# Fused attention and two feed-forward layers: transposes behind later weight loads, another order of seven products, a shorter alternation at the end

## The chip, the cores and the metric

The kernel runs on one core of one Trainium2 chip. The metric is device time in microseconds of one launch; three runs before gave 1210.41, 1207.80 and 1208.92, median 1208.92.

## The reference

What is computed, cut to its core (scale factors of the inputs left out):

```python
# q, k, v: (8, 8, 576, 64); chunks of 64 rows attend to themselves alone
scores = (1/8) * q_c @ k_c.T
attn = exp(scores - max) / (sum + 1e-9)
x = heads_side_by_side(attn @ v_c)              # (4608, 512)
h = x @ w_in                                    # (512, 2048)
x = (h / (1 + exp(-h))) @ w_out                 # (2048, 512)
h = x @ w_in2                                   # (512, 1024)
e = exp(h - max(h)); solu = h * e / (sum(e) + 1e-9)
ln = (solu - mean) / sqrt(var + 1e-6) * g_ln
out = ln @ w_out2                               # (1024, 512)
```

## The kernel before

The 4608 rows are worked in nine blocks of 512. Every factor of a large product is kept as two float16 parts, high and low, and a product is three matmuls: high x high, high x low, low x high. Blocks 0 and 1 run while the weights are still being decoded and split; from block 2 on the large products use a scheme in which four quarter products become seven products of sums (Strassen's), so each layer runs seven products j = 0 to 6 on operands that VectorE, ScalarE and GpSimd prepare, and puts the results together in `combine` (L485). There `a`, `c[0]` and `p` are PSUM banks, named pa, pb and pc in the profile. Product 0 goes into pa and is copied out by ScalarE (L494); product 1 is added on top in pa and copied (L501); product 3 goes into pb and is copied (L498); product 4 goes into pc and is added by VectorE; product 2 goes on top of pa, 6 on top of pb, 5 on top of pa. The order of the seven is a tuple: `HSEQ = (0, 3, 1, 4, 2, 6, 5)` or `XSEQ = (0, 4, 1, 3, 2, 6, 5)`.

A block b from 3 on has these stages on TensorE:

- First half: the first layer for one half of the hidden columns (`h_fast` twice, alternately), 14 products of 12 matmuls (lines L479 to L481), operands x and xb. Each product takes one tile of the weight ring.
- The second layer of the block before for its second pair of row tiles, `m_fast(b - 1, 1)` (L666), alternating with the output product of the first two row tiles, `m_out` (lines L790, L791 and L798).
- Second half: `h_fast` twice again, then `m_out` of the third row tile, and, from here on called the x phase, the seven products of the first layer's second matrix (`x_fast`, lines L580 to L582) with the attention of the next block between them (s_ps, x_ps) and `m_out` of the fourth row tile after the first product.
- Beside the last product of the x phase, piece by piece: `m_fast(b, 0)`, the second layer for the block's own first pair (lines L696 to L698). Its operands are xs[0] = x2q of quarter (0, c), xs[4] and xs[5] = x2q of quarter (1, c), and xs[1], xs[2], xs[3], xs[6] = the sums x2s that VectorE and ScalarE make of both (`x_fast`, L610 to L613, split at L108 and L113).

`m_fast` ends in `m_norm` (L728), the softmax and layer norm of a pair of row tiles: exp (L752), its product (L754), squares (L760), a power on GpSimd (L767), scaling (L770), the two parts of u (L771 on ScalarE, L772 on VectorE), and then four DMA transposes uT<-u (L776) on the sync queue, two for each row tile. `m_out` reads uT.

The weight ring (`Ring`, L438) holds eight tiles of 256 KB. After each product `load` issues the load of the tile that goes into the slot just freed (L449). The loads, the transposes and all other DMAs named here are issued by SyncE, in the order in which they stand in its program; one that waits holds those behind it. A block takes 56 ring tiles: 28 of the first matrix (w1s) and 28 of the second (w2s). The order of instructions on each engine is found by a scheduler from the order in the code, dependences and priorities.

At the end, after the last block, `m_fast(8, 1)` alternates with the rest of the third output tile and the whole fourth one of block 7; then the four output tiles of block 8 follow.

Of the kernel before, what the change touches and what calls it, by code (L numbers as in the profile page):

```python
# [16 lines left out]
P = 128  # L17
# [29 lines left out]
def fused(ctx: ExitStack, tc: tile.TileContext, qkv, w1, w2, w3, w4, g_ln, out):  # L47
    nc = tc.nc
    V, A, G, T = nc.vector, nc.scalar, nc.gpsimd, nc.tensor
# [13 lines left out]
    MO = (0, 1, 2, 3)  # L63
# [3 lines left out]
    EXB = [6, 7, 10, 13, 14]  # L67
    PHA = [4, 5, 6, 7, 8, 10, 11, 15, 32, 33, 34, 35]
    QF = 14

    const = ctx.enter_context(tc.tile_pool(name="const", bufs=1))
    one = ctx.enter_context(tc.tile_pool(name="one", bufs=1))
# [340 lines left out]
    UL = V  # L413
# [13 lines left out]
    def w2_sums(c, q):  # L427
        ys = [one.tile([P, 2, 4, P], F32, tag=f"q{10 + i}", name="y") for i in range(2)]

        def staging():  # L430
# [4 lines left out]
        sums((w2t[c, q], w2t[c, 2 + q], w2t[2 + c, q], w2t[2 + c, 2 + q]),  # L435
             lambda j: dst[j], [ys[i // 2][:, i % 2] for i in range(4)], staging)

    class Ring:  # L438


# [4 lines left out]
        def load(self):  # L445
            while self.n < min(self.used + self.depth, self.count):
                shape, src = self.src(self.n)
                t = one.tile(shape, F16, tag=f"{self.tag}_{self.n % self.depth}", name="ring")
                nc.sync.dma_start(out=t, in_=src)  # L449
                self.tiles.append(t)  # L450
                self.n += 1

        def take(self):
            self.used += 1
# [10 lines left out]
    HSEQ = (0, 3, 1, 4, 2, 6, 5)  # L465
# [18 lines left out]
    def combine(h, shape, seq, product, done, add, c21_first=False):  # L484

        a, c = bank(shape, "pa"), {}  # L490
        for j in seq:
            if j == 0:
                product(j, a, True)
                A.activation(h[0], a, AF.Copy)  # L494
            elif j == 3:
                c[0] = bank(shape, "pb")
                product(j, c[0], True)
                A.activation(h[3], c[0], AF.Copy)  # L498
            elif j == 1:
                product(j, a, False)  # L500
                A.activation(h[1], a, AF.Copy)  # L501
            elif j == 4:
                p = bank(shape, "pc")
                product(j, p, True)
                add(0, h[0], p)
                done(0, 0, h[0])
            elif j == 2:
                product(j, a, False)
                add(3, h[3], a)
                done(1, 1, h[3])  # L510
            elif j == 6:
                product(j, c[0], False)
                add(1, h[1], c[0])
                if c21_first:
                    done(1, 0, h[1])
            else:
                product(j, a, False)
                done(0, 1, a)
                if not c21_first:
                    done(1, 0, h[1])  # L520
            yield

    def run(*parts):

        parts = list(parts)
        while parts:
            for g in list(parts):
                if next(g, parts) is parts:
                    parts.remove(g)
# [147 lines left out]
    def m_fast(b, c, alt=False):  # L677

        e, tags = [], []
        for i in range(2):  # L680
            if b < NB - 1:
                tags.append(e_tag(ns[0]))
                ns[0] += 1
            else:
                tags.append(f"q{4 + 2 * c + i}")
            e.append(one.tile([P, F2], F32, tag=tags[i], name="e"))
        z = xq.pop((b, 2, c))
        x0, x1 = xq.pop((b, 0, c)), xq.pop((b, 1, c))
        a, d = slice(0, P), slice(P, HB)
        xs = ([x0[:, i, :, a] for i in range(2)], [y[:, 1] for y in z], [y[:, 0] for y in z], [y[:, 2] for y in z],  # L690
              [x1[:, i, :, a] for i in range(2)], [x1[:, i, :, d] for i in range(2)], [y[:, 3] for y in z])

        def product(j, ps, start):
            (h, l), w = xs[j], w3s[j]
            for k in range(2):
                T.matmul(ps, h[:, k], w[:, 0, k], start=start and k == 0, stop=False, skip_group_check=True)  # L696
                T.matmul(ps, h[:, k], w[:, 1, k], start=False, stop=False, skip_group_check=True)
                T.matmul(ps, l[:, k], w[:, 0, k], start=False, stop=k == 1, skip_group_check=True)  # L698


        y = [e[i // 2][:, i % 2 * 512:i % 2 * 512 + 512] for i in range(4)]


        part = sml.tile([P, 2], F32, tag="mp", name="mp")
        m = sml.tile([P, 2], F32, tag="mm_", name="mm_")

        def add(n, out, p, own=True):
            i = n // 2
            first = n in (0, 3)
            V.tensor_tensor_reduce(  # L710
                out=out, in0=p, in1=out if own else zero.to_broadcast([P, 512]), scale=1.0,
                scalar=LEAST if first else part[:, i:i + 1], op0=ALU.add, op1=ALU.max,
                accum_out=(part if first else m)[:, i:i + 1])

        def done(r, k, x):
            if (r, k) == (0, 1):
                add(2, y[2], x, own=False)

        yield from combine(y, [P, 512], HSEQ, product, done, add)
        u_tags, uT_tags = ["m1", "w3_10"], [tags[0] if c else "m2", tags[1]]  # L720
        if alt:
            u_tags, uT_tags = ["q0", "q2"], ["q1", "q3"]
        elif not more_(b):
            uT_tags = ["q10", "q11"]
        m_norm(b, [2 * c, 2 * c + 1], [[(e[i], slice(0, F2))] for i in range(2)], m, e, u_tags, uT_tags,
               G if alt else UL)

    def m_norm(b, ts, parts, m, es, u_tags, uT_tags, eng_l=V):  # L728

        n, np = len(ts), len(parts[0])  # L730
        us_ = [one.tile([P, 2, F2], F16, tag=x, name="u") for x in u_tags]
        small = lambda tag: sml.tile([P, n], F32, tag=f"{tag}{n}", name=tag)
        inv = 1.0 / (S_X2 * S_W)

        def joined(tag, one_part):

            r = sml.tile([P, n * np], F32, tag=f"{tag}{n}", name=tag)
            for i in range(n):
                for k, (y, c) in enumerate(parts[i]):
                    one_part(i, y, c, r[:, i * np + k:i * np + k + 1])  # L740
            if np == 1:
                return r
            z = sml.tile([P, n], F32, tag=f"{tag}j", name=tag)
            V.tensor_reduce(out=z, in_=r, axis=AX.X, op=ALU.add)
            return z

        nm = small("nm")
        for i in range(n):
            V.tensor_scalar(out=nm[:, i:i + 1], in0=m[:, i:i + 1], scalar1=-inv, scalar2=None, op0=ALU.mult)
        ex = [u.rearrange("p h f -> p (h f)").bitcast(F32) for u in us_]  # L750
        s = joined("s", lambda i, y, c, r: exps.append(
            A.activation(ex[i][:, c], y, AF.Exp, scale=inv, bias=nm[:, i:i + 1], accum_out=r).ins))  # L752

        us = joined("us", lambda i, y, c, r: V.scalar_tensor_tensor(  # L754
            out=es[i][:, c], in0=y, scalar=1.0, in1=ex[i][:, c], op0=ALU.mult, op1=ALU.mult, accum_out=r))
        nmu = small("nmu")
        V.tensor_scalar(out=nmu, in0=us, scalar1=-1.0 / F2, scalar2=None, op0=ALU.mult)
        dv = small("dv")
        for i in range(n):
            A.activation(ex[i], es[i], AF.Square, bias=nmu[:, i:i + 1], accum_out=dv[:, i:i + 1])  # L760


        V.tensor_scalar(out=s, in0=s, scalar1=1e-9, scalar2=1.0 / inv, op0=ALU.add, op1=ALU.mult)
        c = small("c")
        V.scalar_tensor_tensor(out=c, in0=s, scalar=1e-6 / S_LN ** 2, in1=s, op0=ALU.mult, op1=ALU.mult)
        V.scalar_tensor_tensor(out=c, in0=dv, scalar=1.0 / F2 / S_LN ** 2, in1=c, op0=ALU.mult, op1=ALU.add)  # L766
        G.tensor_tensor(out=c, in0=c, in1=mhalf.to_broadcast([P, n]) if n > 1 else mhalf, op=ALU.pow)  # L767
        for i in range(n):
            e, u = es[i], us_[i]
            V.tensor_scalar(out=e, in0=e, scalar1=nmu[:, i:i + 1], scalar2=c[:, i:i + 1], op0=ALU.add, op1=ALU.mult)  # L770
            A.activation(u[:, 0, :], e, AF.Copy)  # L771
            eng_l.tensor_tensor(out=u[:, 1, :], in0=e, in1=u[:, 0, :], op=ALU.subtract)  # L772
            uT = one.tile([P, 2, K2, P], F16, tag=uT_tags[i], name="uT")
            ut[b, ts[i]] = uT[:, 0], uT[:, 1]
            for h in range(2):
                nc.sync.dma_start_transpose(out=uT[:, h], in_=u[:, h])  # L776

    def in_turn(*parts):
        for g in parts:
            yield from g  # L780
# [207 lines left out]

    b = NB - 1
    run(begun)  # L990
    run(m_fast(b, 1), in_turn(m_out(b - 1, MO[2], high=False), m_out(b - 1, MO[3])))
    for t in MO:
        run(m_out(b, t))

# [46 lines left out]
```

## Time and profile before

| | |
|---|---|
| median of the timed runs | 1208.92 us (1207.80 to 1210.41) |
| the profiled execution | 1211.81 us |
| its span, first to last instruction | 1210.0 us |
| TensorE busy | 1137.6 us (94%) |
| VectorE busy | 906.0 us (75%) |
| ScalarE busy | 805.5 us (67%) |
| mean granted TensorE clock | 0.978 of full speed |

The times in the views count from the start of the span. "Idle before" an instruction is the time its engine stood still, with what released it. PE is TensorE, DVE VectorE, ACT ScalarE, POOL GpSimd, SP SyncE; a q behind the name is the engine's queue.

### The profile page before, as it was taken

Reading aid. Unit: us, or ns where it says so; the run is one execution under the profiler, and the core shown is the slowest. Engines: PE = TensorE matmul, PEld = TensorE weight load, DVE = VectorE, ACT = ScalarE, POOL = GpSimd, SP = SyncE. Lnnn points to the kernel's source line nnn. Section 1 sums busy time; section 2 is a strip of 40 time slices with the busy share of each in tenths; the row PEclk is TensorE's granted clock in tenths of the full one; section 3 lists DMA queues with packets and bytes.
Section 4 is the critical chain, followed back from the end, with each engine's and each line's share of the span. In section 5 each row is a group of like instructions: output and inputs, shape, how many; then the busy total and the mean of one; then the engine's idle time right before and its main releaser. Section 6 shows DMA issues by size and latency. Waiting matters only on the chain. (4 is left out here: it accounts for less than half of the span.)

```text
span 1210.0 us, 23575 instructions
## 1 busy us (share of the span) xinstructions
PE 1137.6 (94%) x9036; PEld 770.7 (64%) x9036; DVE 906.0 (75%) x1638; ACT 805.5 (67%) x1475; POOL 251.8 (21%) x241
## 2 busy tenths in 40 slices
PE   4997889988999989999999999999999999999998
PEld 4444434444557766787678766867677767777853
DVE  5888986568587788788878887778688867886343
ACT  7777767766577668746875687558755875587243
POOL 3356423224201430032003200311021102100001
PEclk7898979999999999999999999999999999999999
DMA  8778643444446655676567666666666667564704
GB/s 290 247 228 247 202 144 104 128 152 131 128 110 199 180 170 157 183 207 186 158 183 207 187 157 183 194 184 163 168 200 199 166 150 216 176 157 138 205 15 113
DMA packets 205169, 209.18 MB, mean 173 GB/s; under 512 B 120192, under 2 KB 130432, under 8 KB 205056
## 3 DMA queue, kind: packets, MB, share of 16 engines
q1 hardware_dynamic: 205056, 207.68, 59.0%
q8 instruction: 70, 1.15, 0.4%
q14 instruction: 43, 0.35, 0.1%
HBM read 156.24 MB, written 24.12 MB: 149 GB/s over the span
## 5 line engine op out<-in xcount | busy, mean ns | idle before, releaser
L113 DVE SCALAR_TENSOR_TENSOR q<-hc,q 128x512 f16<-128x512 f32 x196 | 137.9, 719 | 12.5 <-ACT q L108 10.3
L108 ACT ACTIVATE q<-hc 128x512 f16<-128x512 f32 x196 | 120.2, 626 | 38.0 <-DVE hc L561 12.1
L112 POOL TENSOR_TENSOR qbl<-qk,qbh 64x512 f16<-64x512 f32 x58 | 79.7, 1374 | 283.0 <-ACT qbh L108 237.0
L580 PE MATMUL pa<-q,ring 128*128 128x256 f16 x448 | 122.7, 274 | 0.0
L581 PE MATMUL pa<-q,ring 128*128 128x256 f16 x448 | 122.7, 274 | 0.0
L582 PE MATMUL pa<-q,ring 128*128 128x256 f16 x448 | 122.7, 274 | 0.0
L790 PE MATMUL o_ps<-w4h,uT 128*128 128x512 f16 x288 | 109.2, 379 | 1.7 <-DMA uT<-u 1.7
L791 PE MATMUL o_ps<-w4l,uT 128*128 128x512 f16 x288 | 109.2, 379 | 0.0
L767 POOL TENSOR_TENSOR c<-c,mhalf 128x2 f32<-128x2 f32 (+1 forms) x22 | 14.1, 642 | 396.9 <-DVE c L766 396.9
L479 PEld LDWEIGHTS <-ring 128*128 128x128 f16 x784 | 77.0, 98 | 20.3 <-DMA ring<-w1s 9.7
L480 PEld LDWEIGHTS <-ring 128*128 128x128 f16 x784 | 77.0, 98 | 15.0 <-issue 4.5
L581 PEld LDWEIGHTS <-ring 128*128 128x128 f16 x784 | 76.9, 98 | 11.5 <-issue 0.3
L580 PEld LDWEIGHTS <-ring 128*128 128x128 f16 x784 | 76.9, 98 | 11.3
L481 PEld LDWEIGHTS <-ring 128*128 128x128 f16 x784 | 77.0, 98 | 9.1
L582 PEld LDWEIGHTS <-ring 128*128 128x128 f16 x784 | 76.9, 98 | 9.2
L798 PE MATMUL o_ps<-w4h,uT 128*128 128x512 f16 x288 | 70.3, 379 | 0.0
L479 PE MATMUL pa<-xb,ring 128*128 128x256 f16 x224 | 61.1, 273 | 8.9 <-DMA ring<-w1s 7.6
L479 PE MATMUL pa<-x,ring 128*128 128x256 f16 x224 | 61.3, 274 | 2.1 <-ACT hc L494 2.1
L481 PE MATMUL pa<-x,ring 128*128 128x256 f16 x224 | 61.5, 274 | 0.0
L480 PE MATMUL pa<-x,ring 128*128 128x256 f16 x224 | 61.3, 274 | 0.0
L479 PE MATMUL pb<-x,ring 128*128 128x256 f16 x224 | 61.1, 273 | 0.2 <-DMA ring<-w1s 0.2
L580 PE MATMUL pb<-q,ring 128*128 128x256 f16 x224 | 61.1, 273 | 0.0
(264 smaller groups left out, 3484.5 us busy)
## 6 DMA issues: line engine op xcount, KB each, us to landing
ring<-w1s SPq DMA_DIRECT2D x196, 256.0 KB, 3.3
ring<-w2s SPq DMA_DIRECT2D x196, 256.0 KB, 3.8
wst<-w SPq DMA_DIRECT2D x48, 512.0 KB, 4.9
qk<-qkv SPq DMA_DIRECT2D x29, 512.0 KB, 3.8
vs<-qkv SPq DMA_DIRECT2D x36, 256.0 KB, 3.1
out<-o SPq DMA_DIRECT2D x36, 256.0 KB, 2.1
w1s<-ws SPq DMA_DIRECT2D x32, 128.0 KB, 1.8
w2s<-ws SPq DMA_DIRECT2D x16, 256.0 KB, 2.0
```

What stands on the lines that cost most here:

```text
L108: A.activation(dst_h, src, AF.Copy, scale=scale)
L112: return G.tensor_tensor(out=dst_l, in0=src, in1=dst_h, op=ALU.subtract).ins
L113: return V.scalar_tensor_tensor(out=dst_l, in0=src, scalar=scale, in1=dst_h, op0=ALU.mult, op1=ALU.subtract).ins
L479: T.matmul(ps[:, c], wh, x[:, 0, k], start=first, stop=False, skip_group_check=True)
L480: T.matmul(ps[:, c], wh, x[:, 1, k], start=False, stop=False, skip_group_check=True)
L481: T.matmul(ps[:, c], wl, x[:, 0, k], start=False, stop=k == 1, skip_group_check=True)
L580: T.matmul(ps[:, c], wh, g[:, 0], start=first, stop=False, skip_group_check=True)
L581: T.matmul(ps[:, c], wh, g[:, 1], start=False, stop=False, skip_group_check=True)
L582: T.matmul(ps[:, c], wl, g[:, 0], start=False, stop=q == 1 and f == 3, skip_group_check=True)
L790: T.matmul(ps, uh[:, k], w4h[:, k, :], start=k == 0, stop=False)
L791: T.matmul(ps, uh[:, k], w4l[:, k, :], start=False, stop=False)
L798: T.matmul(ps, ul[:, k], w4h[:, k, :], start=False, stop=k == K2 - 1)
```

## The change

Three edits. First, for the second pair of a block (not of the last one) `m_norm` no longer issues the transposes where it stands; it puts them on a list `late`, and the ring issues the first tile's two right behind the load with which its count has grown by seven, and the second tile's two behind the load after that. Second, `m_fast` runs its seven products in the order XSEQ where it had HSEQ. Third, at the end `m_fast(8, 1)` alternates with the rest of the third output tile alone, and the fourth one comes behind it.

```diff
+    DEFER = 7
...
+    late = []
...
-                nc.sync.dma_start(out=t, in_=src)
+                i = nc.sync.dma_start(out=t, in_=src).ins
                 self.tiles.append(t)
                 self.n += 1
+                if late and late[0][0] <= self.n:
+                    with tc.issue_after(i):
+                        late.pop(0)[1]()
...
-        yield from combine(y, [P, 512], HSEQ, product, done, add)
+        yield from combine(y, [P, 512], XSEQ, product, done, add)
...
         m_norm(b, [2 * c, 2 * c + 1], [[(e[i], slice(0, F2))] for i in range(2)], m, e, u_tags, uT_tags,
-               G if alt else UL)
+               G if alt else UL, DEFER if c and more_(b) else 0)
...
-            for h in range(2):
-                nc.sync.dma_start_transpose(out=uT[:, h], in_=u[:, h])
+
+            def turn(u=u, uT=uT):
+                for h in range(2):
+                    nc.sync.dma_start_transpose(out=uT[:, h], in_=u[:, h])
+
+            if defer:
+                late.append((ring.n + defer, turn))
+            else:
+                turn()
...
-    run(m_fast(b, 1), in_turn(m_out(b - 1, MO[2], high=False), m_out(b - 1, MO[3])))
+    run(m_fast(b, 1), m_out(b - 1, MO[2], high=False))
+    run(m_out(b - 1, MO[3]))
```

In the second half of a block the sync queue held this before (the last ring<-w1s_99 is the last tile of the first matrix; the uT are of the second pair):

```order
L449 DMA ring<-w1s_98 128x1024
L449 DMA ring<-w1s_99 128x1024
L449 DMA ring<-w1s_98 128x1024
L449 DMA ring<-w1s_99 128x1024
L449 DMA ring<-w1s_98 128x1024
L776 DMA_TRANSPOSE uT<-u 128x8x128 x4
L449 DMA ring<-w1s_99 128x1024
L449 DMA ring<-w2s_100 128x1024
L449 DMA ring<-w2s_101 128x1024
```

and with the change (L452 is the old L449, L784 the old L776):

```order
L452 DMA ring<-w1s_98 128x1024
L452 DMA ring<-w1s_99 128x1024
L452 DMA ring<-w1s_98 128x1024
L452 DMA ring<-w1s_99 128x1024
L452 DMA ring<-w1s_98 128x1024
L452 DMA ring<-w1s_99 128x1024
L452 DMA ring<-w2s_100 128x1024
L784 DMA_TRANSPOSE uT<-u 128x8x128 x2
L452 DMA ring<-w2s_101 128x1024
L784 DMA_TRANSPOSE uT<-u 128x8x128 x2
L452 DMA ring<-w2s_102 128x1024
```

The last w1 load and the first w2 load now stand ahead of the four transposes, and one more w2 load stands between the two pairs of them.

On ScalarE, beside the last product of the last x phase, the copies of the second layer (e<-pa, e<-pb) and the splits x2q and x2s stood so:

```order
L108 ACTIVATE x2s<-xt 128x1024
L494 ACTIVATE e<-pa 128x512
L498 ACTIVATE e<-pb 128x512
L501 ACTIVATE e<-pa 128x512
L599 ACTIVATE xc_14103<-pa 128x512
L108 ACTIVATE x2q<-xc_14103 128x2x128
L108 ACTIVATE x2s<-xt 128x1024
L494 ACTIVATE e<-pa 128x512
L752 ACT_TABLE_LOAD
```

and stand so with the change (L500 is the old L494, L504 the old L498, L507 the old L501, L605 the old L599, L109 the old L108, L758 the old L752):

```order
L109 ACTIVATE x2s<-xt 128x1024
L500 ACTIVATE e<-pa 128x512
L507 ACTIVATE e<-pa 128x512
L605 ACTIVATE xc_14103<-pa 128x512
L109 ACTIVATE x2q<-xc_14103 128x2x128
L504 ACTIVATE e<-pb 128x512
L109 ACTIVATE x2s<-xt 128x1024
L758 ACT_TABLE_LOAD
```

The copy of pb, which is that of product 3, comes later, and the table load no longer stands behind the copy of the next pair's product 0.

On the sync queue at the very end, behind the last ring load, there stood:

```order
L449 DMA ring<-w2s_103 128x1024
L804 DMA out<-o 128x512
L776 DMA_TRANSPOSE uT<-u 128x8x128 x4
L804 DMA out<-o 128x512 x2
L776 DMA_TRANSPOSE uT<-u 128x8x128 x4
L804 DMA out<-o 128x512 x3
```

and now stands:

```order
L452 DMA ring<-w2s_103 128x1024
L817 DMA out<-o 128x512
L784 DMA_TRANSPOSE uT<-u 128x8x128 x4
L817 DMA out<-o 128x512
L784 DMA_TRANSPOSE uT<-u 128x8x128 x4
L817 DMA out<-o 128x512 x4
```

One output tile has moved from ahead of the last four transposes to behind them.

## Rows read from the trace of the kernel before

**Rows 1.** The page's part 1: busy us (share of the span) and instructions.
```profile
PE 1137.6 (94%) x9036; PEld 770.7 (64%) x9036; DVE 906.0 (75%) x1638; ACT 805.5 (67%) x1475; POOL 251.8 (21%) x241
```

**Rows 2.** TensorE's waits, 330 to 1210 us: us, times, longest.
```profile
PE pa L479 <- DMA ring<-w1s: 7.6, 6, 1.9
PE pb L698 <- DVE x2s L113: 4.1, 7, 0.8
PE x_ps L250 <- DMA pT<-ae: 3.2, 4, 1.3
PE pb L696 <- ACT x2s L108: 1.9, 2, 1.7
PE o_ps L790 <- DMA uT<-u: 1.7, 1, 1.7
PE pa L479 <- DVE hc L532: 1.4, 5, 0.3
```

**Rows 3.** Clock of a stretch; timelines (start, us) of ScalarE and TensorE.
```profile
806.00:809.40 3.40, 3.40 (x15) 2.11 (x14) 1.64 (x3) 0.97 (x2) 0.00 (x0) 0.50 0.21 77
...
802.18 0.63 ACT L108 ACTIVATE vbh<-vs 64x512 f16<-64x512 f32 x1 [2.39 <-DMA vs<-qkv]
...
804.12 0.39 PE L696 MATMUL pb<-w3s,x2s 128*128 128x512 f16 x1 [1.66 <-ACT x2s L108]
...
805.38 0.39 PE L698 MATMUL pb<-w3s,x2s 128*128 128x512 f16 x1 [0.66 <-DVE x2s L113]
```

**Rows 4.** Timeline of TensorE, second half of a block.
```profile
977.42 0.27 PE L479 MATMUL pa<-xb,ring 128*128 128x256 f16 x1
...
996.08 0.28 PE L479 MATMUL pa<-xb,ring 128*128 128x256 f16 x1 [1.46 <-DMA ring<-w1s]
```

**Rows 5.** Timeline of the sync queue, the same stretch.
```profile
986.74 6.10 SPq L776 DMA_TRANSPOSE uT<-u  x4
992.93 0.53 SPq L449 DMA_DIRECT2D ring<-w1s  x1
993.55 4.36 SPq L449 DMA_DIRECT2D ring<-w2s  x8
```

**Rows 6.** The transposes from 331 us: ns min/median/max; landing in us.
```profile
L776 SPq DMA_TRANSPOSE uT<-u x54: 1237/1261/2517, 333.0 to 1112.3; - x54
...
DMA to landing us min/median/max: 2.7/2.8/5.6
```

**Rows 7.** Timelines of VectorE and TensorE, end of an x phase.
```profile
1046.79 0.68 DVE L113 SCALAR_TENSOR_TENSOR x2q<-xc,x2q 128x512 f16<-128x512 f32 x1
...
1049.66 1.22 DVE L113 SCALAR_TENSOR_TENSOR x2s<-xt,x2s 128x1024 f16<-128x1024 f32 x1
...
1050.93 0.39 PE L698 MATMUL pb<-w3s,x2s 128*128 128x512 f16 x1 [0.78 <-DVE x2s L113]
```

**Rows 8.** Timelines of VectorE and TensorE, first half of a block.
```profile
950.55 2.35 DVE L772 TENSOR_TENSOR u<-e,u 128x1024 f16<-128x1024 f32 x2
954.04 0.69 DVE L113 SCALAR_TENSOR_TENSOR q<-hc,q 128x512 f16<-128x512 f32 x1 [0.54 <-ACT q L108]
954.65 1.28 DVE L532 TENSOR_TENSOR hc<-pa,hc 128x512 f32<-128x512 f32 x2
...
955.38 0.27 PE L479 MATMUL pa<-xb,ring 128*128 128x256 f16 x1 [0.25 <-DVE hc L532]
```

**Rows 9.** Timeline of TensorE, the end.
```profile
1182.94 0.38 PE L698 MATMUL pa<-w3s,x2q 128*128 128x512 f16 x1
1183.80 0.38 PE L790 MATMUL o_ps<-w4h,uT 128*128 128x512 f16 x1
...
1195.98 0.39 PE L790 MATMUL o_ps<-w4h,uT 128*128 128x512 f16 x1 [1.66 <-DMA uT<-u]
```

**Rows 10.** Timeline of VectorE in an x phase.
```profile
1025.78 0.69 DVE L209 TENSOR_REDUCE am<-s_ps 128x8 f32<-128x512 f32 x1 [2.87 <-PE s_ps L207]
```

More of the change, by code (lines that the diff above doesn't have):

```diff
@@ L725, in m_fast, with m_norm @@
         m_norm(b, [2 * c, 2 * c + 1], [[(e[i], slice(0, F2))] for i in range(2)], m, e, u_tags, uT_tags,
-               G if alt else UL)
-    def m_norm(b, ts, parts, m, es, u_tags, uT_tags, eng_l=V):
+               G if alt else UL, DEFER if c and more_(b) else 0)
+    def m_norm(b, ts, parts, m, es, u_tags, uT_tags, eng_l=V, defer=0):
         n, np = len(ts), len(parts[0])
```

## The prediction

> **What bounds the kernel now.** I read the page first: TensorE is busy for 1137.6 us (94% of the span) and VectorE for 906.0 (75%) [rows 1]. So the kernel is bound by TensorE, no matmul is added or taken away by this change, and what it can win is TensorE's idle time alone. The second view was therefore the list of TensorE's waits from 330 us on, where the long loop over blocks runs [rows 2]. The reader is to see that this list is short, about 20 us, and that four kinds of entries in it belong to the three edits: six waits for a w1 tile of the weight ring (7.6 us), nine for the operand x2s of the second layer (4.1 + 1.9 us), five for an hc (1.4 us), one for uT (1.7 us). The wait for pT of the attention (3.2 us) belongs to none. Then I went to one place of each kind in the timelines.
>
> The third view was the granted clock in three stretches around 806 us [rows 3]: 0.50 there, which is the 1.2 GHz level, for 3.40 us. Just before, TensorE had stood still for 1.66 us (behind ScalarE's x2s, which itself came late because the vbh in front of it waited 2.39 us for a vs to land). It is the only drop between 331 us and the last microsecond that I found, and it costs half of 3.40, 1.7 us.
>
> **Part 1, the transposes behind later loads.** In the second half of a block TensorE eats one ring tile per (994.62 - 977.42) / 13 = 1.32 us, from 977.42 until it stops before the last of fourteen; it goes on at 996.08, 1.46 us late, when that tile has landed [rows 4]. The sync queue shows why [rows 5]: four transposes held it for 6.10 us from 986.74, and only at 992.93 the load of that last tile was issued, 3.1 us before it was used (996.08). Its slot had been free since about 977.42 + 6 x 1.32 = 985.3. In the changed order that load stands before the transposes. It would be issued at about 985.5 and land, by the same 3.1 us, near 988.6, some 6 us before TensorE asks at 994.6. So the six waits go: -7.6 us.
>
> What is moved must be paid for. The transposes now wait for one more load, the first w2 tile; its slot is free at 977.42 + 7 x 1.32 = 986.7, so they start near 987.1, 0.4 us later. They land after 2.8 us (median [rows 6]), near 990, and the first reader, the third output tile, stands on TensorE after the fourteen products, at about 994.6 + 1.3 = 995.9. The second tile's two transposes follow behind one more load and are read by the fourth output tile, behind the scores and the whole first x product. The cover is thus 6 us, and if it were gone each microsecond of lateness would cost six. The w2 loads behind them start at about 993.3 where they started at 993.55 [rows 5], so what the x phase reads lands as before. The first pair's transposes are not deferred; one of them now stands ahead of one ring load, which TensorE does not read before the next half (u is made at 950.55, the half starts at 977.42 [rows 4, 8]): nothing. The bounds of this part are 0 (the wait returns elsewhere) and -7.6; I take -7.6, since the queue row and the wait row end at the same load.
>
> A rule speaks against this part. The Trainium skill, page "Advanced Engine Details and Errata", section "X-Bar Transpose (TRN2)", says that transposing DMAs are as fast as regular ones. By it the four would hold the queue like four loads, 4 x 4.36 / 8 = 2.2 us, the late tile would have been in time, and moving it would be worth nothing; the sum below would be 7.6 us smaller. The trace does not agree on the queue's side: a transpose holds it for 1.26 us in the median, a load for 4.36 / 8 = 0.55 us; only the landings are alike (2.8 us [rows 6] and 3.1 us).
>
> **Part 2, the second layer's product order.** Before, the second of seven products needs the low part of x2s, which VectorE ends at 1049.66 + 1.22 = 1050.88, and TensorE stands for 0.78 us [rows 7]. In the changed order the second product needs only x2q, done at 1046.79 + 0.68 = 1047.47, 2 us before it is asked for (that product's first two matmuls ended at 1050.93 - 0.78, so it began near 1049.6); x2s is wanted by the third, one product and one x piece later (2.6 us), at about 1052.2, against 1050.88. So the wait goes and 1.3 us of slack is left. In the worst block the two waits are 1.66 and 0.66, together 2.32, still below 2.6 [rows 2, 3]. All nine: -6.0 us, and the clock's drop with its cause: -1.7 us. What may become late instead: the fourth product's bank is now accumulated on again after only one product (1.3 us), and ScalarE must have copied it by then, 0.6 us plus the hand-over; I keep about 0.5 us of slack there and price it at nothing, with up to 0.5 us in each of seven passes, 3.5 us, as the other end.
>
> The new order also moves work on VectorE in the first half of the next block. The row of L532 at 954.65 ends TensorE's 0.25 us wait [rows 8]; before it stands a q split of 0.69 us that waited 0.54 us for ScalarE, and that split now stands behind the hc additions. So that L532 comes some 0.6 us earlier and the five waits go: -1.4 us. For ScalarE's copies in the pair that follows I counted as many instructions ahead of the first as before (sixteen), so nothing is added there. Bounds 0 and -1.4.
>
> **Part 3, the end.** The last product of the second pair ends at about 1183.9; from there to the matmul that waits for uT, at 1195.98 [rows 9], runs a chain of addition, normalization and transpose of 12.0 us, covered by two output tiles of 24 matmuls at 0.215 us (four from 1182.94 to 1183.80), 10.3 us; the wait is 1.66 us. Changed, 13 of the 24 matmuls of the older output tile stand behind the pair instead of inside it. The chain starts 13 x 0.215 = 2.8 us earlier for the same end of TensorE's work, so the wait is covered with 1.1 us to spare. Against it: the first pair's normalization shares VectorE and ScalarE with the pair's additions there, and TensorE may stand up to 0.5 us for a copy. I take -1.2 us; bounds +0.5 and -1.7.
>
> **Sum.** 7.6 + 6.0 + 1.7 + 1.4 + 1.2 = 17.9 us off the profiled execution's own 1211.81 gives 1193.9. That execution is 2.9 us above the median of the timed runs, 1208.92, and I hold the late vs of rows 3 for the cause: 1.5 us of its wait above the 0.78 of an ordinary block, and the 1.7 of the clock. Without these 3.2 the sum is 14.7, and 1208.9 - 14.7 = 1194.2. Both roads meet; I forecast 1194.
>
> **Rivals.** *The ring's wait returns.* TensorE comes 1.5 us earlier to the attention and the x phase, and something there is no earlier: VectorE, three quarters busy overall, or a load. For it: a wait for pT stands in the list already [rows 2]. Against: VectorE waits 2.87 us for TensorE's scores at 1025.78 [rows 10], so its chain moves along. Part 1 lost: 14.7 - 7.6 = 7.1, and 1208.9 - 7.1 = 1201.8. (By the rule of the Trainium skill above the time would end there too.) *The order does not do what it says*: x2s is late for the third product as it was for the second, because both come from the same x at the end of the sixth product. Against: 1050.88 is before 1052.2. Part 2's 4.5 lost: 1198.7. *Slower: the deferred transposes come too late.* They now wait in an in-order queue for a slot that TensorE must free. From a start after 993.1 on (987.1 + 6) the third output tile stands still in six blocks; at 996.3 it is 3.2 us each, 19 us, against 14.7 won: 1213. Against: the slot is freed by the seventh of fourteen products, long before.
>
> **How the numbers follow.** Forecast 0.72 (its own range 1191 to 1198); ring wait returns 0.12; second layer's wait stays 0.07; slower 0.05; the rest, a gain of less than 0.2% from several small new waits, 0.04. A measurement of this kernel can tell about 0.2%, 2.4 us, from no change. That gives 0.91 faster, 0.04 within, 0.05 slower. The range goes from 1190 (all bounds at their good end, and some of the pT waits too) to 1202, which takes in the first two rivals.
>
> **What would show it.** In the changed trace: no wait of L479's line for a ring tile in the six blocks, the last w1 load issued before the transposes; no wait of the second layer for x2s; the hc waits gone; at the end no wait for uT; the clock at 1.00 from 331 us on; TensorE's busy time unchanged. I am wrong if TensorE's idle time after 330 us is still above 12 us, and above all if o_ps waits for uT in the blocks or x_ps for pT more than 5 us in all.

## The result and the profile after

The changed kernel takes 1192.98 us, median of four runs (1190.54 to 1193.78), against 1208.36 for the kernel before beside it (1207.06 to 1210.41): 15.4 us less, a ratio of 0.9876, 95% interval 0.9857 to 0.9895. The profiled execution took 1193.78 us with a span of 1192.0, 18.0 less than the one before. The predicted 1194 (1190 to 1202, faster) was right; its account was only partly so.

The page's part 1, which answers to [rows 1]:

```profile
PE 1132.0 (95%) x9036; PEld 771.7 (65%) x9036; DVE 907.3 (76%) x1638; ACT 802.8 (67%) x1475; POOL 247.0 (21%) x241
```

TensorE's waits from 330 us on (us, times, longest), which answer to [rows 2]; these four are all that the view lists:

```profile
PE pa L485 <- ACT hc L507: 4.1, 5, 0.9
PE x_ps L251 <- ACT xb L109: 3.0, 3, 1.6
PE x_ps L251 <- DMA pT<-ae: 2.0, 2, 1.7
PE x_ps L253 <- DVE vbl L114: 1.6, 2, 1.4
```

The waits for ring, x2s and uT are gone, as forecast. But the place of the five waits for an hc (the tile into which ScalarE copies a product of the first layer, and to which VectorE adds the others), 1.4 us that should have gone, is taken by five others for an hc, 4.1 us, with ScalarE behind them. The wait for xb and pT is one wait with two names: whichever of the two the view names, TensorE goes on 0.04 to 0.14 us after pT has landed. It was 3.2 + 0.3 us before and is 5.0 now.

The two parts of the span (start:end, length, busy time of PE, PEld, DVE, ACT and POOL; the third number from the end is the granted clock), of before:

```profile
0.00:330.00 330.00, 283.36 (x1835) 146.01 (x1836) 246.82 (x452) 228.30 (x490) 129.47 (x132) 0.93 0.58 181
330.00:1210.00 880.00, 854.23 (x7203) 624.71 (x7201) 659.19 (x1186) 577.17 (x987) 122.36 (x109) 1.00 0.60 170
```

and of after:

```profile
0.00:330.00 330.00, 284.33 (x1842) 147.32 (x1843) 247.57 (x454) 228.79 (x491) 130.19 (x133) 0.95 0.58 182
330.00:1192.00 862.00, 847.62 (x7196) 624.40 (x7193) 659.72 (x1185) 573.99 (x984) 116.79 (x108) 1.00 0.62 173
```

From 330 us on idle time went from 880 - 854.2 = 25.8 to 862 - 847.6 = 14.4 us, 11.4 less; 3.5 us of each lie behind TensorE's last matmul. Busy time fell by 6.6, 1.0 of it because seven more matmuls ran ahead of 330 us; over the whole span, with the same 9036 matmuls, it fell by 5.6. So some two thirds of the 18.0 us are idle time; where the rest is from stands under the steps below.

On the sync queue, second half of a block (answers to [rows 5]):

```profile
967.43 6.30 SPq L452 DMA_DIRECT2D ring<-w1s  x6
974.72 0.32 SPq L452 DMA_DIRECT2D ring<-w2s  x1
975.13 2.87 SPq L784 DMA_TRANSPOSE uT<-u  x2
```

The last w1 load, the sixth of the first row, now stands ahead of the transposes. The transposes and their landing in this stretch (answers to [rows 6]):

```profile
L784 SPq DMA_TRANSPOSE uT<-u x4: 1237/1268/1577, 975.1 to 980.6; - x4
...
DMA to landing us min/median/max: 3.3/4.2/5.2
```

and their first reader on TensorE, which did not wait:

```profile
983.70 0.38 PE L803 MATMUL o_ps<-w4h,uT 128*128 128x512 f16 x1
```

The first transpose took the 5.2 us and landed at 980.3: the cover, the time from its landing to its first reader, is 3.4 us here and 4.4 to 4.9 in the other five blocks, not the 6 that the prediction gave it from a landing of 2.8. The first of the four landed 2.7 us after its start in each of the six blocks before, and 3.6 to 5.2 us after it in the changed kernel.

End of the x phase on VectorE and TensorE (answers to [rows 7]): x2s ends at 1037.13, its reader, now the third product, starts at 1038.23 and does not wait; 1.1 us of slack, 1.3 were forecast.

```profile
1035.91 1.22 DVE L114 SCALAR_TENSOR_TENSOR x2s<-xt,x2s 128x1024 f16<-128x1024 f32 x1
...
1038.23 0.38 PE L702 MATMUL pa<-w3s,x2s 128*128 128x512 f16 x1
```

First half of a block (answers to [rows 8]), ScalarE, TensorE and VectorE:

```profile
935.26 0.58 ACT L507 ACTIVATE hc<-pa 128x512 f32<-128x512 f32 x1
936.85 2.00 ACT L777 ACTIVATE u<-e 128x1024 f16<-128x1024 f32 x2 [1.00 <-DVE e L776]
938.76 0.58 ACT L507 ACTIVATE hc<-pa 128x512 f32<-128x512 f32 x1
...
939.39 0.27 PE L485 MATMUL pa<-x,ring 128*128 128x256 f16 x1 [0.77 <-ACT hc L507]
...
940.22 1.28 DVE L538 TENSOR_TENSOR hc<-pc,hc 128x512 f32<-128x512 f32 x2
941.41 0.68 DVE L538 TENSOR_TENSOR hc<-pa,hc 128x512 f32<-128x512 f32 x1
```

Read them in this order: VectorE's additions follow each other as forecast, with no q split between (a split makes the high and the low part of the tile that it is named after). But on ScalarE two u splits now stand ahead of the second copy of pa; they wait 1.00 us for e, run 2.00 us, and TensorE, which wants to add on that bank again, stands 0.77 us. Before, both copies stood ahead of the u splits:

```profile
947.81 1.07 ACT L501 ACTIVATE hc<-pa 128x512 f32<-128x512 f32 x2
949.40 2.00 ACT L771 ACTIVATE u<-e 128x1024 f16<-128x1024 f32 x2 [0.52 <-DVE e L770]
```

The second edit did that, far from where it is made (e2_order below).

### The profile page after: what moved, and what is told of

Its sections match the earlier page's. It is cut to its first block, busy times and chain, and to the rows that moved or that the text cites. A ratio compares the mean times of both kernels' runs of the same rounds, so it can differ in the third digit from the quotient of the medians.

```text
span 1192.0 us, 23579 instructions
## 1 busy us (share of the span) xinstructions
PE 1132.0 (95%) x9036; PEld 771.7 (65%) x9036; DVE 907.3 (76%) x1638; ACT 802.8 (67%) x1475; POOL 247.0 (21%) x241
## 4 chain that ended last, share of the span: by engine, by line
PE 61%; DVE 12%; ACT 11%; DMA 8%; issue 5%; POOL 2%; SPq 0%; ACTq 0%; POOLq 0%; DVEq 0%
PE o_ps L804 5%; PE o_ps L811 5%; PE o_ps L803 5%; PE pa L588 3%; PE pa L586 3%; PE pa L587 3%; PE pa L485 3%; PE pa L487 3%; PE pa L486 3%; DMA wst<-w 3%; DMA vs<-qkv 2%; DVE vbl L114 2%; DMA qk<-qkv 2%; PE pa L704 2%; PE pa L702 2%
## 5 line engine op out<-in xcount | busy, mean ns | idle before, releaser
L109 ACT ACTIVATE q<-hc 128x512 f16<-128x512 f32 x196 | 119.1, 624 | 41.6 <-DVE hc L573 16.3
L113 POOL TENSOR_TENSOR qbl<-qk,qbh 64x512 f16<-64x512 f32 x58 | 75.3, 1298 | 266.8 <-ACT qbh L109 225.4
L485 PEld LDWEIGHTS <-ring 128*128 128x128 f16 x784 | 76.9, 98 | 10.9 <-DMA ring<-w1s 0.2
L485 PE MATMUL pb<-x,ring 128*128 128x256 f16 x224 | 61.1, 273 | 0.0
L487 PE MATMUL pb<-x,ring 128*128 128x256 f16 x224 | 61.1, 273 | 0.0
```

Of the source, the lines that this page charges most:

```text
L109: A.activation(dst_h, src, AF.Copy, scale=scale)
L113: return G.tensor_tensor(out=dst_l, in0=src, in1=dst_h, op=ALU.subtract).ins
L485: T.matmul(ps[:, c], wh, x[:, 0, k], start=first, stop=False, skip_group_check=True)
L487: T.matmul(ps[:, c], wl, x[:, 0, k], start=False, stop=k == 1, skip_group_check=True)
```

## The experiments

Ratios are to the kernel before, run beside each kernel.

**Each edit alone.** The first edit, with all its lines of the diff above, and no other:

```diff
+    DEFER = 7
...
+                if late and late[0][0] <= self.n:
```

> Only the first edit (the second pair's transposes behind later weight loads); order of the seven products and end as before. Theory (the waits of TensorE add up): the six ring waits of 7.6 us go, nothing takes their place, and each stop that is no longer made gives back another 0.16 us, the part of the last matmul that no follower overlaps: 7.6 + 6 x 0.16 = 8.6, so 1199.8 against a before of 1208.4. ScalarE's order in the first half stays that of before, so five waits for hc of 0.25 to 0.33 us stay. Rival 1 (the idle time alone counts): 1200.8. Rival 2 (the ring's wait returns at another load or at pT): within 2 us of 1208.

Measured: 0.9935 (0.9913 to 0.9958), 7.9 us less of 1208.

```profile
PE pb L704 <- DVE x2s L114: 3.9, 6, 0.8
PE x_ps L251 <- DMA pT<-ae: 3.8, 4, 1.8
PE x_ps L251 <- ACT xb L109: 1.8, 2, 1.6
...
PE pa L485 <- DVE hc L538: 1.5, 5, 0.4
```

No ring wait is left in the list, the hc waits stay; pT and xb together are 5.6 us (3.5 before), but a second execution of the old blocks has 4.9 (e3_end below), so that it isn't shown that anything came back there. The theory's 0.993 lies within the interval, and so does rival 1, the idle time alone, at 0.994: this run cannot tell the two apart.

The second edit:

```diff
-        yield from combine(y, [P, 512], HSEQ, product, done, add)
+        yield from combine(y, [P, 512], XSEQ, product, done, add)
```

> Only the second edit (product order of the second layer). Theory: the nine x2s waits go, 6.0 us in the profiled execution, some 4.5 in an ordinary one, with 9 x 0.16 = 1.5 us for the stops; but ScalarE's second hc copy now stands behind the two u splits, so the five hc waits grow from 1.4 to 4.1 us: net -6.0 to -4.5, -1.5, +2.7, so -3.3 to -4.8: 1203.6 to 1205.1. Rival, as the prediction had it (hc waits go too): -4.5 - 1.4 - 14 x 0.16 = -8.1, 1200.3. Rival (x2s late for the third product): 1208. The ring waits stay at 7 to 8 us in all three.

Measured: 0.9968 (0.9953 to 0.9984), 3.9 us less, as the theory has it; the prediction's account, which the text above gives as 8, is out, and so is an x2s that is late for the third product. The ring waits, for which I had 7 to 8 us, are 5.8 in this profile.

```profile
PE pa L479 <- DMA ring<-w1s: 5.8, 5, 1.8
PE pa L479 <- ACT hc L501: 4.3, 5, 1.0
```

The hc waits on ScalarE come with this edit alone, and x2s is in no row.

The third edit:

```diff
-    run(m_fast(b, 1), in_turn(m_out(b - 1, MO[2], high=False), m_out(b - 1, MO[3])))
+    run(m_fast(b, 1), m_out(b - 1, MO[2], high=False))
+    run(m_out(b - 1, MO[3]))
```

> Only the third edit (the end). Theory: the one wait for uT near the end goes, 1.66 us and 0.16 for the stop: -1.8, 1206.6; the blocks before it are unchanged, hc waits of 0.25 us and all ring and x2s waits included. Rival (the copies of the pair that follow each other faster stop TensorE as long): 1208.4.

Measured: 1.0015 (0.9996 to 1.0034): no gain that can be told; my theory of -1.8 missed. The rows:

```profile
PE pa L479 <- DMA ring<-w1s: 6.5, 6, 1.8
PE x_ps L250 <- DMA pT<-ae: 4.0, 4, 1.6
...
PE o_ps L790 <- DMA uT<-u: 1.0, 1, 1.0
PE x_ps L250 <- ACT xb L108: 0.9, 2, 0.7
...
PE pa L696 <- ACT e L501: 0.2, 1, 0.2
```

Of the 1.7 us for uT, 1.0 stays and 0.2 is new: with the old product order a copy stops TensorE in the closer pair. On VectorE, in the chain that ends in that uT, the same operation on two tiles stands so:

```profile
1179.02 1.23 DVE L754 SCALAR_TENSOR_TENSOR e<-e,u 128x1024 f32<-128x1024 f32 x1 [1.29 <-ACT u L752]
...
1180.17 3.14 DVE L754 SCALAR_TENSOR_TENSOR e<-e,u 128x1024 f32<-128x1024 f32 x1
```

The second took 1.9 us more than the first, and TensorE waited 1.0, so that in this execution the wait hangs on that instruction. Why it took so long is open, and with it whether the third edit needs the second.

Until 1172 us every engine of e3_end does the same instructions in the same order as before, so that its profile is a second execution of the old blocks. Its ring waits are 6.5 us where the first execution had 7.6, those for x2s 4.4 where it had 6.0, those for pT and xb 4.9 where it had 3.5. So much do rows of one profile differ without an edit.

**Edits undone in the changed kernel.** First edit undone:

```diff
-    DEFER = 7
+    DEFER = 0
```

> The changed kernel with its first edit undone (transposes where they stood). Theory, the effects add up: the six ring waits come back as in the kernel before, 7.6 us and 6 x 0.16, less what e1_defer measured short of that: +7.9, a ratio of 0.994, 1201. Rival (with the second edit TensorE comes to the ring earlier, so the waits are longer): 0.997 or more. Rival (the second edit already took part of the ring waits): 0.991 or less.

Measured: 0.9941 (0.9919 to 0.9964). Against 0.9876 that is 7.9 us, as the edit alone gave: the effects add up, and both rivals' figures lie outside the interval. In its profile the ring waits are shorter than before, so part of the 7.9 is not in this row:

```profile
PE pa L485 <- DMA ring<-w1s: 5.0, 6, 1.5
```

Third edit undone (the last diff but one, backwards):

> The changed kernel with its third edit undone (the end alternates as before). Theory: the uT wait of 1.7 us comes back, with 0.16 for the stop: 1.8 above the changed kernel, 1194.8 or a ratio of 0.989. Rival, from e3_end (the third edit is worth at most 0.5 us by itself): the uT wait is 1.0 or less and the time that of the changed kernel, 0.9876.

Measured: 0.989 (0.9869 to 0.991). The interval holds both answers, so that the time tells nothing; the row decides: the wait is back in full, and in the changed kernel there is none.

```profile
PE o_ps L803 <- DMA uT<-u: 1.7, 1, 1.7
```

**The copy on ScalarE.** An edge puts the first pair's u splits behind the second copy:

```diff
+            s_ins = A.activation(u[:, 0, :], e, AF.Copy).ins
+            ... held.append(s_ins)
...
+                while hold and held:
+                    tc.add_manual_dep(held.pop(0), i.name, NOSYNC, ...)
```

> The changed kernel with one more edge: the u splits of the first pair stand behind ScalarE's last copy for hc (the order that the kernel before had there). Theory: the five waits for that copy (4.1 us, and 5 x 0.16 for the stops) go, but VectorE's order of before comes back with it, one q split ahead of the hc additions, and with it five waits of about 0.27 us (and 5 x 0.16): -4.1 + 1.4 = -2.7, 1190.3 against 1193.0 of the changed kernel (on the ratio to before: 0.985). If the copies' place is not the cause: 1193.

Measured: 0.9848 (0.9823 to 0.9874), 18.4 us less. This interval overlaps that of the changed kernel (0.9857 to 0.9895), so that the gain over it is not shown by the time; the rows tell.

```profile
PE pa L486 <- DVE hc L541: 2.0, 5, 0.7
```

The five waits for the copy that was L507 are gone and those for VectorE are back, as expected; two of 0.5 us for the copy of product 0 (L501 of this kernel) stand in its list too. So a second edge puts the first q split behind the hc additions (`first_q` holds that split, `i` is the addition of the second of the two products):

```diff
+                i = add(3, h[3], a)
+                while hold and first_q:
+                    tc.add_manual_dep(first_q.pop(0), i.name, NOSYNC, ...)
```

> The kernel of v2_held with a second edge: on VectorE the first q split of a block stands behind the additions for hc that follow the u splits. Theory: the five waits of TensorE for hc <- DVE that v2_held shows (0.41, 0.28, 0.21, 0.72, 0.37, in sum 2.0) go, with 5 x 0.16 for the stops: 2.8 off v2_held's ratio of 0.985, so 0.9825 or 1187; no wait for hc from 450 us on. Rival (the q split only moves the wait to a later hc): as v2_held.

Measured: 0.9826 (0.9802 to 0.985), 21 us less than before, the lowest ratio of the study; this interval lies wholly below that of the changed kernel. No wait for hc is listed from 450 us on (two of 0.5 us stand ahead of 370). The other waits from 330 us on are the attention's:

```profile
PE x_ps L251 <- ACT xb L109: 2.3, 3, 1.6
PE x_ps L251 <- DMA pT<-ae: 1.9, 3, 0.8
PE x_ps L253 <- DVE vbl L114: 1.4, 1, 1.4
```

**What lateness costs.** The changed kernel with a later place for the transposes:

```diff
-    DEFER = 7
+    DEFER = 12
```

> The changed kernel with the transposes of the second pair behind the load with which the ring has grown by twelve, not seven: measures the price of lateness. Theory (the sync queue in order, a slot freed every 1.30 us): they start about 981.5 in a block whose second half begins at 965.4 and land 2.8 us later, at 984.3, against a first reader at 983.6: a wait for uT of 0.7 us in six blocks, with 6 x 0.16: 5 us, 1198. Rival (the transposes are not in the way of anything, landing is what counts, hidden by other work): 1193. Rival (the prediction's point, a start after 993.1 on its clock, was too early): 1193 too, with no uT wait in the rows.

Measured: 1.0003 (0.9987 to 1.0019), 15 us above the changed kernel, three times what I expected; the six waits are 12.0 us, 2.0 each and not 0.7. Timelines of the queue and of TensorE in one block:

```profile
990.47 2.72 SPq L784 DMA_TRANSPOSE uT<-u  x2
...
994.48 0.39 PE L803 MATMUL o_ps<-w4h,uT 128*128 128x512 f16 x1 [1.83 <-DMA uT<-u]
```

and the landing of its four transposes:

```profile
DMA to landing us min/median/max: 3.4/3.7/4.0
```

They start where the theory put them (16.3 us into the second half), but the first of a block's four lands after 3.9 to 4.2 us, not 2.8; here too a load stands right ahead of it in the queue. That is most of the 1.3 us by which each wait exceeds the theory's 0.7.

And with `DEFER = 13`:

> As e5_d12, with thirteen. Theory: one product later, 1.3 us more in each of six blocks: a wait of 2.0 us in each, 13 us in all, 1206. Rival (lateness is hidden): 1193.

Measured: 1.0102 (1.0079 to 1.0124), 27 us above the changed kernel, twice what I expected. Six waits, 19.1 us:

```profile
PE o_ps L803 <- DMA uT<-u: 19.1, 6, 3.5
```

and after two of the six the clock fell to its lower level, 1.2 GHz, for 3.4 us, which costs 1.7 each (the second of these stretches, behind the longest stop, 3.52 us, shows none):

```profile
507.50:510.90 3.40, 3.23 (x8) 1.19 (x9) 3.40 (x7) 1.68 (x4) 0.00 (x0) 0.51 1.15 232
755.30:758.70 3.40, 3.39 (x16) 1.58 (x17) 3.40 (x7) 1.89 (x3) 0.00 (x0) 1.00 1.10 249
879.60:883.00 3.40, 3.22 (x8) 1.19 (x9) 3.40 (x7) 1.68 (x4) 0.00 (x0) 0.50 1.15 229
```

**The waits that are left.** Edges that put the attention's exponential (`soft[-1]`) ahead of vbh, and of the copy of x_ps in the same way:

```diff
+                with tc.issue_after(soft[-1]):
+                    split(vh[r, :, r], vl[r, :, r], v[r], S_V, A, V)
```

> The kernel of v3_both with more edges: in blocks 4 to 8 ScalarE's exponential of the attention stands ahead of the split vbh and of the copy of x_ps, which stood ahead of it. It tests what is behind the waits for pT and xb that are left (0.85, 0.21, 0.40, 1.59, 0.46, 0.64 us in v3_both). Theory: the exponential waits in ScalarE's queue behind a vbh whose vs has not landed (ScalarE stands 4.06 us at 780.69, the exponential follows at 781.99), so the chain to pT moves 0.5 to 1.3 us forward where vs is late, and the pT waits of blocks 4 on (2.7 in v3_both, with 4 x 0.16) go; against it vbl comes later and a wait of 0.4 us for vbl may appear in each of five blocks, -2: net -3.3 to -1, a ratio of 0.980 to 0.9815. Rival (pT is held by something else): as v3_both, 0.9826, or slower by the vbl waits, 0.984.

Measured: 0.987 (0.9848 to 0.9893): the theory's 0.980 to 0.9815 is out and so, just, is the rival's 0.984. It is slower than v3_both by 0.0044, though the two intervals touch (0.9848 and 0.985). ScalarE in v3_both:

```profile
780.69 1.28 ACT L109 ACTIVATE vbh<-vs 64x512 f16<-64x512 f32 x2 [4.06 <-DMA vs<-qkv]
781.99 0.63 ACT L220 ACTIVATE ae<-ae 128x512 f32<-128x512 f32 x1
```

and in this kernel:

```profile
778.89 0.63 ACT L225 ACTIVATE ae<-ae 128x512 f32<-128x512 f32 x1 [3.16 <-DVE ae L224]
```

TensorE's waits in it:

```profile
PE x_ps L258 <- DVE vbl L114: 5.7, 7, 1.4
PE x_ps L256 <- DMA pT<-ae: 1.7, 3, 1.2
PE x_ps L256 <- ACT xf L333: 1.5, 2, 0.9
```

The exponential comes 3.1 us earlier, 0.9 of it because TensorE is that much earlier at this place in this execution. What is won at pT and xb (4.2 to 3.2 us; the two put down to L333 end 0.13 us after pT has landed, so they are counted with pT) is lost at vbl: 5.7 - 1.4 = 4.3 us more, where I had 2.

## Why the prediction was right, step by step

In the profiled executions (predicted, then measured; us):

| step | predicted | measured |
|---|---|---|
| ring waits | -7.6 | -7.8 |
| x2s waits | -6.0 | -6.0 |
| hc waits | -1.4 | +2.7 |
| uT at the end | -1.2 | -1.7 |
| clock | -1.7 | -1.7 |
| waits for pT, xb, vbl | 0 | +1.5 |
| stops, beyond their idle time (an estimate, below) | not in the sum | -2.9 |
| before 330 us, idle | 0 | -1.0 |
| rest, busy time | 0 | -1.1 |
| sum | -17.9 | -18.0 |

Not all signs that the prediction named came out. TensorE's idle time after 330 us, which was not to stay above 12 us, is 14.4, or 10.9 without the 3.5 behind its last matmul; x_ps waits 5.0 us for pT, the very limit; the hc waits are not gone, and TensorE's busy time did not stay the same but fell by 5.6.

**Part 1** was right in mechanism and size; alone and undone it is worth 7.9 us. By the rule of the Trainium skill, page "Advanced Engine Details and Errata", section "X-Bar Transpose (TRN2)", that transposing DMAs are as fast as regular ones, moving the transposes would have been worth nothing, as the prediction worked out; the runs say otherwise, so of the two the row on the queue was the one to trust. What was mis-sized is its cover, 3.4 to 4.9 us and not 6, because the transposes land later behind the load that now stands ahead of them. The rival "slower" was so nearer than I had it: not from a start at 993.1 but 1.1 to 2.6 us earlier; by the 1.31 us of a tile that is an estimate of ten or eleven tiles, where the prediction's 6 us would be twelve. e5_d12 and e6_d13, at twelve and thirteen, pay 2.0 and 3.2 us in each block.

**Part 2** was right for x2s and wrong for hc. The step that failed: "For ScalarE's copies in the pair that follows I counted as many instructions ahead of the first as before (sixteen), so nothing is added there." I counted for the pair's copies and not for hc's, one row further on the same engine. That cost 4.1 us of waits; v2_held and v3_both show it in their rows, by taking the waits away. VectorE's part of the forecast came true as an order (no q split between the additions) and was hidden by it; that they come 0.6 us earlier was not measured apart. The other end of the bounds, a stop for the fourth product's bank (copied in L504), stands in no list of waits.

**Part 3** was right in the changed kernel, where the wait of 1.7 us is gone (1.2 forecast). Alone it gave nothing that can be told (e3_end); whether that is the old product order or the one long VectorE instruction is open.

**The clock** dropped in no profile of e1_defer, e2_order or e3_end near 806 us. e1_defer and e3_end keep the waits for x2s, and none of theirs is above 0.9 us, so that the drop belonged to that one execution, in which the x2s behind the late vs stopped TensorE for 1.66 us; its -1.7 is no gain of an edit in an ordinary execution. Taking it and the late vs out of the median's sum fits what was measured, 15.4 for 14.7.

**Why the sum held** all the same: what hc and pT took (5.6 us off the forecast) is about what stops gave back (2.9) and the last rows of the table (2.1). That these cancel is luck: none of them was in the sum. A stop costs more than its idle time. Of before, at the wait of [rows 8]:

```profile
954.86 0.27 PE L481 MATMUL pb<-x,ring 128*128 128x256 f16 x1
955.38 0.27 PE L479 MATMUL pa<-xb,ring 128*128 128x256 f16 x1 [0.25 <-DVE hc L532]
```

Without a stop a matmul follows the one before after 0.11 us; here it follows after 0.52, 0.41 late, of which 0.25 count as idle and 0.16 as the busy end of the last matmul. From 330 us on, 31 stops of over 0.06 us became 13: 18 x 0.16 = 2.9, an estimate that no run tests by itself. The first 2024 matmuls, which no edit touches, took 361.7 us before and 360.2 in this execution, with a granted clock of 0.93 and 0.96; that is chance or a shift, and was not tried apart. The 1.5 us more at pT, xb and vbl are not shown to be an effect of the edits: e3_end, with the old blocks, has 6.5 us there and the changed kernel 6.6. What sets these waits stays open: the vs loads landed 2.5 to 4.8 us after their issue before and 2.5 to 4.6 in the changed kernel, and v5_exp did not settle it.

## What to carry to other kernels

A DMA that holds an in-order queue is worth putting behind the loads that have a deadline, as long as its own landing, measured behind those loads, still leaves cover. When an order of products changes, compare the order of each engine at every place where the engine that bounds the kernel waits, not only where the edit is; a swap on ScalarE cost 4.1 us of waits here. Price a stop at its idle time plus the end of the last matmul that no follower overlaps, 0.16 us here. And profile the same kernel twice before a change of a microsecond in one row is put down to an edit.

## What the runs showed of the hardware

The first transpose of the second pair landed 2.7 us after its start in all six blocks before, and 3.6 to 5.2 us after it in the changed kernel, 3.9 to 4.2 in e5_d12, where a plain load stood right ahead of it in the queue; with the edit undone (r1_nodefer) it was 2.7 to 2.8 again. Single transposes before took up to 5.6 us too [rows 6]. In e6_d13 stops of TensorE of 3.30 and 3.14 us were followed by 3.4 us at 1.2 GHz, and one of 3.52 us was not.
